# Attention outputs in two passes per block: one head's high and low value parts as weights, its high and low probabilities as the moving side, and the sum of the halves on VectorE

## The chip, the cores and the metric

The kernel runs on one core of a Trainium2 chip. The metric is the device time of one execution in microseconds (us). The three timed runs took 1136.36, 1138.24 and 1138.36 us; their median, 1138.24 us, is the time before.

Engines are named as in the profile: PE is TensorE's matrix multiplication, PEld its loading of weights, DVE is VectorE, ACT is ScalarE, POOL is GpSimd, and SP issues the DMAs.

## What is computed

A windowed attention over 8 batches, 8 heads, 576 positions and 64 features per head, followed by a gated feed-forward layer on the 4608 rows of 512 features:

```python
scores = scale * q @ k.T                   # per batch and head, scale 1/8
mask_plain = (rel >= 0) & (rel < 32)       # heads 0 to 3
mask_dil = (rel >= 0) & (rel < 128) & (rel % 4 == 0)   # heads 4 to 7
attn = softmax(where(mask, scores, -1e9))
out = attn @ v                             # [8, 8, 576, 64]
x = out.transpose(0, 2, 1, 3).reshape(4608, 512)
xn = x / sqrt(mean(x * x) + 1e-6) * rms_g
g = xn @ w_gate;  val = xn @ w_val         # d_ff = 1536
y = (g * sigmoid(g) * val) @ w_out
```

The change concerns the line `out = attn @ v` only.

## The kernel before

The rows are cut into 16 units (u = 0 to 15) of 288 rows, half a batch each. A unit goes through two stages. Its attention comes first: four pairs of heads c, two heads a in each, and per pair three blocks of 96 queries (c = 0, 1, plain window) or four of 72 queries (c = 2, 3, dilated), which are 14 blocks i per unit. Then comes its feed-forward layer: for each of 12 column groups j a gate product (`g`), a value product (`v`) and an output product (into four accumulators `acc`). The attention of a unit is spread over the feed-forward steps of the unit before it, so that TensorE always has large products to run.

**Precision.** Units 0 and 1 multiply in full fp32. From unit 2 on (NNAT = 2) every fp32 number is split in a high and a low part of the type fp32r, and a product is the sum of high by high, high by low and low by high.

**The order of the work** is written out by hand. One step of the loop is one large product (gate, value or output; 12 matmuls of 288 columns for a full one) plus the attention parts that `plan` puts there. `later(dt, rank, fn)` puts a piece of work for the other engines into the step dt ahead, and within a step the pieces are issued by rank. Every engine then runs its own instructions in that order.

**A block's way** (from unit 3 on two steps lie between a block and the next; in unit 2 the blocks come in pairs of neighbouring steps):

1. `scored` (line 499 before): scores into the PSUM bank `s`. 
2. `scores_max` (lines 366 and 371, DVE), `scores_exp` (381, ACT), `scores_norm` (390 and 391, DVE; 397, POOL).
3. `transposed` (469, PE): the probabilities are transposed into the free columns of a bank that also serves gate and value products (`g`, `v`, or a tile `t` of its own in one of these two banks). `untranspose` copies them out in the next step as `pt`, the high part on ACT (452) and the low part on DVE (454). The bank's next product must wait for both.
4. `output` (483, 487, 488, PE): probabilities by values into the bank `o`. Once the opening of the kernel is over there is one such bank.
5. `take` (417, ACT) copies a result from the bank into `xraw`, and `add` (427, DVE, rank 4 of its step) adds another to it. The next block's `output` must wait until the bank has been read.

Before the change the values of both heads are the weights together: `vhi` and `vlo`, [keys, 2 heads x 64]. The moving side holds both heads' probabilities. For a unit of 3 to 15 a block needs two matmuls. Line 487 multiplies `vhi` by high and low probabilities of both heads, 4 x 96 = 384 or 4 x 72 = 288 columns, and line 488 multiplies `vlo` by the high ones of both, 192 or 144 columns, on top of the high half. Of the 128 output rows by all columns only the two blocks in which value head and probability head agree are used. `take` reads the low-probability half of them and `add` the other, two instructions of 64 rows each. In unit 2 a block has three matmuls (line 483) that all add up in the same 192 or 144 columns, `take` alone reads the result, and there is no `add`.

`split_v` makes the value parts, `vhi` on ACT (306) and `vlo` on POOL (310). For unit 2's blocks, DVE also splits the feed-forward weights for the units to come (`split_weight`, lines 247 and 248). Line 349 makes the low part of the queries, 613 that of the layer's input, 676 and 689 are the gate's arithmetic on DVE, 700 and 701 split its result, 723 writes out finished results. The feed-forward products are lines 632, 633 and 634.

## Time and profile before

| What | Value |
|---|---|
| timed runs, median | 1138.24 us |
| profiled execution, first to last instruction | 1137.1 us |
| granted TensorE clock, mean | 0.997 |
| PE busy | 1119.5 us, 98% |
| DVE busy | 795.5 us, 70% |
| ACT busy | 708.7 us, 62% |
| POOL busy | 615.7 us, 54% |
| blocks whose outputs change | 14 in unit 2; 182 in units 3 to 15 (78 of 96 queries, 104 of 72) |

The profile is of a single execution whose span is 1.1 us under the median of the timed runs. A row of a timeline reads: start, duration, engine, line, operation, what is written and read, shape, count, and in brackets how long the engine sat idle before and who ended that. A matmul's duration contains its way through the array, and the next one starts long before it ends. How much of TensorE's time one takes is therefore read from the distance between starts, not from its duration.

### The profile page before, as it was taken

To read this page: it belongs to the slowest core of one execution; us is meant where nothing else is said; L and a number is where in the kernel's file an instruction comes from. 1 tells how busy PE (TensorE), PEld (TensorE's weight loads), DVE (VectorE), ACT (ScalarE), POOL (GpSimd) and SP (SyncE) were. 2 spreads that over 40 slices of the span, in tenths; PEclk is the share of its full clock that TensorE was granted. 3 is DMA by queue.
4 is the path that set the end of the run, shared out by engine and by line. 5 is a ranking of instruction groups with operands and counts; after the bars stand their busy time and mean duration, and the time that the engine had idled before them with its cause. 6 is when DMAs were issued, how large, how long until landed. Compare 5 with 4: busy or idle time off the path is not lost.

```text
span 1137.1 us, 25931 instructions
## 1 busy us (share of the span) xinstructions
PE 1119.5 (98%) x8371; PEld 1088.7 (96%) x8371; DVE 795.5 (70%) x2875; ACT 708.7 (62%) x2608; POOL 615.7 (54%) x1071
## 2 busy tenths in 40 slices
PE   9999889999999999999999999999999999999998
PEld 7787779999999999999999999999999999999998
DVE  6889878858667585876758677675867768586411
ACT  6795665657667566675757666575766757576311
POOL 8223677656556455565646556564655646465311
PEclk9999989999999999999999999999999999999999
DMA  9665221212213031221213122121311212120000
GB/s 246 181 228 198 78 59 40 82 40 71 64 34 98 27 95 42 79 62 31 81 40 103 41 63 74 36 84 39 86 51 54 87 34 79 42 80 15 6 17 22
DMA packets 61545, 82.19 MB, mean 72 GB/s; under 512 B 7298, under 2 KB 41090, under 8 KB 61410
## 3 DMA queue, kind: packets, MB, share of 16 engines
q1 hardware_dynamic: 61410, 80.54, 23.7%
q8 instruction: 67, 1.10, 0.4%
q14 instruction: 68, 0.56, 0.2%
HBM read 71.08 MB, written 9.44 MB: 71 GB/s over the span
## 4 chain that ended last, share of the span: by engine, by line
PE 91%; DVE 5%; ACT 1%; issue 1%; DMA 1%; POOL 1%; POOLq 0%; SPq 0%; ACTq 0%
PE acc L632 9%; PE v L632 8%; PE g L632 8%; PE acc L633 8%; PE acc L634 8%; PE v L633 8%; PE g L633 8%; PE v L634 8%; PE g L634 8%; PE s L499 3%; PE o L487 3%; PE acc L629 2%; PE v L629 1%; PE o L488 1%; PE busy L749 1%; PE g L629 1%
## 5 line engine op out<-in xcount | busy, mean ns | idle before, releaser
L701 POOL TENSOR_TENSOR hlo<-th,hhi 128x288 fp32r<-128x288 f32 x180 | 146.3, 813 | 200.9 <-ACT hhi L700 150.6
L634 PE MATMUL acc<-hhi,lo 128*128 128x288 f32 x720 | 212.6, 295 | 0.0
L397 POOL TENSOR_SCALAR t<-t,sum 72x72 f32<-72x72 f32 (+3 forms) x414 | 153.1, 382 | 69.7 <-DVE sum L391 61.1
L634 PE MATMUL v<-xhi,lo 128*128 128x288 f32 x612 | 180.5, 295 | 0.0
L634 PE MATMUL g<-xhi,lo 128*128 128x288 f32 x612 | 180.3, 295 | 0.0
L700 ACT CAST hhi<-th 128x288 fp32r<-128x288 f32 x180 | 78.1, 434 | 155.7 <-DVE th L689 153.4
L381 ACT ACTIVATE t<-t,sum 96x128 f32<-96x128 f32 (+3 forms) x448 | 166.1, 375 | 11.4 <-DVE sum L371 10.9
L310 POOL TENSOR_TENSOR vlo<-vt,vhi 128x128 fp32r<-128x128 f32 x196 | 94.1, 480 | 107.6 <-ACT vhi L306 92.7
L671 ACT ACTIVATE th<-g 128x288 f32<-128x288 f32 x180 | 73.8, 410 | 106.1 <-PE g L634 86.3
L634 PEld LDWEIGHTS acc<-hhi,lo 128*128 128x128 f32 x720 | 135.9, 189 | 0.0
L427 DVE TENSOR_TENSOR xraw<-o,xraw 64x72 f32<-64x72 f32 (+1 forms) x364 | 99.1, 272 | 50.6 <-ACT xraw L417 44.5
L676 DVE SCALAR_TENSOR_TENSOR th<-th,g 128x288 f32<-128x288 f32 x180 | 80.4, 447 | 68.3 <-ACT th L671 68.3
L634 PEld LDWEIGHTS v<-xhi,lo 128*128 128x128 f32 x612 | 115.4, 189 | 0.0
L634 PEld LDWEIGHTS g<-xhi,lo 128*128 128x128 f32 x612 | 115.2, 188 | 0.0
L632 PE MATMUL g<-xhi,hi_g 128*128 128x288 f32 x357 | 111.0, 311 | 0.1
L632 PE MATMUL acc<-hhi,hi_o 128*128 128x288 f32 x360 | 111.0, 308 | 0.0
L366 DVE TENSOR_TENSOR t<-s,mask 96x256 f32<-96x256 f32 (+3 forms) x196 | 71.5, 365 | 53.5 <-PE s L499 42.6
L689 DVE TENSOR_TENSOR th<-th,v 128x288 f32<-128x288 f32 x180 | 81.4, 452 | 38.0 <-PE v L634 30.1
L633 PE MATMUL acc<-hlo,hi_o 128*128 128x288 f32 x360 | 107.3, 298 | 0.0
L340 POOL TENSOR_TENSOR ks<-qk,ks 128x288 fp32r<-128x288 f32 (+2 forms) x110 | 104.5, 964 | 0.3 <-ACT ks L335 0.3
L417 ACT COPY xraw<-o 64x72 f32<-64x72 f32 (+1 forms) x364 | 94.1, 259 | 11.7 <-PE o L488 9.6
L633 PE MATMUL g<-xlo,hi_g 128*128 128x288 f32 x322 | 94.9, 295 | 0.0
(192 smaller groups left out, 3597.0 us busy)
## 6 DMA issues: line engine op xcount, KB each, us to landing
qk<-in_qk_dram SPq DMA_DIRECT2D x60, 288.0 KB, 2.8
vt<-in_v_dram SPq DMA_DIRECT2D x196, 64.0 KB, 1.9
qk<-in_qk_dram SPq DMA_DIRECT2D x30, 352.0 KB, 3.0
out_dram<-ot SPq DMA_DIRECT2D x64, 144.0 KB, 1.9
qk<-in_qk_dram SPq DMA_DIRECT2D x30, 304.0 KB, 2.8
raw<-in_w_gate_dram SPq DMA_DIRECT2D x12, 512.0 KB, 4.6
raw<-in_w_val_dram SPq DMA_DIRECT2D x12, 512.0 KB, 4.9
raw<-in_w_out_dram SPq DMA_DIRECT2D x12, 512.0 KB, 4.2
```

What stands on the lines that cost most here:

```text
L310: G.tensor_tensor(out=vl, in0=vs.pop(b), in1=vh, op=ALU.subtract)
L340: ek.tensor_tensor(out=ks[:, 1, :nkt], in0=kr, in1=ks[:, 0, :nkt], op=ALU.subtract)
L381: A.activation(out=t[:nq, a, :n], in_=t[:nq, a, :n], func=AF.Exp, scale=-1.0, bias=sm[:nq, a, 0:1], accum_out=sm[:nq, a, 1:2] if u or i % ...
L397: (V if u == 0 and (c, i) > (NC - 1, 0) else G).tensor_scalar(out=t[:nq, a, :n], in0=t[:nq, a, :n], scalar1=sm[:nq, a, 3:4], scalar2=1.0, ...
L417: A.copy(out=to[a * D:(a + 1) * D], in_=o[a * D:(a + 1) * D, (2 + a) * nq:(3 + a) * nq])
L427: V.tensor_tensor(out=to[rows], in0=o[rows, a * nq:(a + 1) * nq], in1=to[rows], op=ALU.add)
L632: PE.matmul(out, wh[:, cc, :], xh, start=start, stop=False)
L633: PE.matmul(out, wh[:, cc, :], xl, start=False, stop=False)
L634: PE.matmul(out, wl[:, cc, :], xh, start=False, stop=stop)
L676: V.scalar_tensor_tensor(out=t, in0=t, scalar=1.0, in1=g, op0=ALU.add, op1=ALU.mult)
L689: V.tensor_tensor(out=t, in0=t, in1=v_ps[:, :U], op=ALU.mult)
L701: G.tensor_tensor(out=lo, in0=t, in1=hi, op=ALU.subtract)
```

## The change

Weights and moving side are paired by head instead of by part. A tile `vhl` holds, for each head, the high and the low values side by side: [keys, 2 heads, 2 parts, 64]. For head a, the weights are its high and low values (128 columns together), and the moving side is its high and its low probabilities, 2 x 96 = 192 or 2 x 72 = 144 columns. The two matmuls of a block, one per head, write disjoint columns of the bank. In the result, rows 0 to 63 belong to the high values and rows 64 to 127 to the low ones. Three of the four quarters are wanted: high by high, high by low and low by high.

`take` copies high values by high probabilities (rows 0 to 63) of each head. `add` adds high values by low probabilities (rows 0 to 63), and then low values by high probabilities (rows 64 to 127 of the bank, added to the same place). It has four DVE instructions per block where there were two, and the second of each head reads what the first has just written. Unit 2 is treated like the later ones: two matmuls in place of three, and four additions in place of none.

```diff
         def hi():
-                vparts[k] = [late[0].tile([P, 2, D], F32R, name=f"v{p}_{k}", bufs=1) for p in ("hi", "lo")]
-            A.copy(out=vparts[k][0], in_=vs[b])
+                vparts[k] = late[0].tile([P, 2, 2, D], F32R, name=f"vhl_{k}", bufs=1)
+            A.copy(out=vparts[k][:, :, 0], in_=vs[b])
...
         def lo():
-            G.tensor_tensor(out=vl, in0=vs.pop(b), in1=vh, op=ALU.subtract)
+            G.tensor_tensor(out=vp[:, :, 1], in0=vs.pop(b), in1=vp[:, :, 0], op=ALU.subtract)
...
     def take(u, c, i, o):
-        if u <= NNAT:
+        if u < NNAT:
...
-                A.copy(out=to[a * D:(a + 1) * D], in_=o[a * D:(a + 1) * D, (2 + a) * nq:(3 + a) * nq])
+                A.copy(out=to[a * D:(a + 1) * D], in_=o[:D, 2 * a * nq:(2 * a + 1) * nq])
...
     def add(u, c, i, o):
-            V.tensor_tensor(out=to[rows], in0=o[rows, a * nq:(a + 1) * nq], in1=to[rows], op=ALU.add)
+            V.tensor_tensor(out=to[rows], in0=o[:D, (2 * a + 1) * nq:(2 * a + 2) * nq], in1=to[rows], op=ALU.add)
+            V.tensor_tensor(out=to[rows], in0=o[D:, 2 * a * nq:(2 * a + 1) * nq], in1=to[rows], op=ALU.add)
...
         def output(a):
-            if o[0] == NNAT:
-                for k, (vp, t) in enumerate(((vh, 0), (vh, 1), (vl, 0))):
-                    PE.matmul(out, vp, pt[:n, t, :, :nq], start=k == 0, stop=k == 2)
-                return
...
-            PE.matmul(both, vh, pt[:n, :, :, :nq], start=True, stop=False)
-            PE.matmul(out, vl, pt[:n, 0, :, :nq], start=False, stop=True)
+            vp = vparts[everything.index(o) % 2]
+            PE.matmul(o_ps[:, 2 * a * nq:2 * (a + 1) * nq].rearrange("d (t q) -> d t q", t=2),
+                      vp[:n, a].rearrange("k t d -> k (t d)"), pt[:n, :, a, :nq], start=True, stop=True)
...
-            if o[0] > NNAT:
+            if o[0] >= NNAT:
                 later(1, 4, lambda: add(*o, o_ps))
```

Lines behind `add` move: 454 becomes 455, 499 becomes 493, and 632 to 634 become 626 to 628. The matmuls of line 481 stand where 487 and 488 did, and the second addition is line 428.

In the rows below, a number that follows a name tells one buffer from another. On PE, in unit 5, the outputs of the second block of its first pair of heads stand between a value product and the scores of a later block. Before:

```order
L634 MATMUL v_0_4816<-xhi_3_4738,lo_708 128x288
L487 MATMUL o_0_1_4830<-pt_0_1_4731,vhi_1320 128x384
L488 MATMUL o_0_1_4830<-pt_0_1_4731,vlo_1321 128x192
L499 MATMUL s_1_2_4829<-ks_2_4527,qs_2_4562 96x256
L499 MATMUL s_1_2_4829<-ks_3_4560,qs_3_4593 96x256
```

And now:

```order
L628 MATMUL v_0_4914<-xhi_3_4834,lo_708 128x288
L481 MATMUL o_0_1_4928<-pt_0_1_4827,vhl_1319 128x192 x2
L493 MATMUL s_1_2_4927<-ks_2_4623,qs_2_4658 96x256
L493 MATMUL s_1_2_4927<-ks_3_4656,qs_3_4689 96x256
L626 MATMUL acc_0_3939<-hhi_11_4830,hi_g_2234 128x288
```

The place is the same; 384 and 192 columns have become twice 192. On DVE, behind that block, the additions stand between the maxima of one later block's scores and the low probabilities (`pt`) of another. Before:

```order
L371 ISA sum_86 96x1
L427 TENSOR_TENSOR xraw_0_4767<-o_0_1_4830,xraw_0_4767 64x96 x2
L390 TENSOR_REDUCE sum_90<-sum_90 96x2
L391 RECIPROCAL sum_90<-sum_90 96x2
L454 TENSOR_TENSOR pt_1_0_4871<-t_0_4864,pt_1_0_4871 128x192
L723 TENSOR_SCALAR ot_1_4877<-acc_1_3869 128x288
```

And now:

```order
L427 TENSOR_TENSOR xraw_0_4863<-o_0_1_4928,xraw_0_4863 64x96
L428 TENSOR_TENSOR xraw_0_4863<-o_0_1_4928,xraw_0_4863 64x96
L427 TENSOR_TENSOR xraw_0_4863<-o_0_1_4928,xraw_0_4863 64x96
L428 TENSOR_TENSOR xraw_0_4863<-o_0_1_4928,xraw_0_4863 64x96
L390 TENSOR_REDUCE sum_90<-sum_90 96x2
L391 RECIPROCAL sum_90<-sum_90 96x2
L455 TENSOR_TENSOR pt_1_0_4971<-t_0_4964,pt_1_0_4971 128x192
```

Everything behind the additions has two more instructions ahead of it. On DVE in unit 2, at its first block, there was no addition between the low probabilities and a weight's low part (`lo`). Before:

```order
L247 CAST hi_v_1543<-f_839 128x512
L454 TENSOR_TENSOR pt_0_2_1568<-t_1_1561,pt_0_2_1568 128x192
L248 TENSOR_TENSOR lo_1506<-f_839,hi_v_1543 128x512
L390 TENSOR_REDUCE sum_88<-sum_88 96x2
L391 RECIPROCAL sum_88<-sum_88 96x2
```

And now:

```order
L455 TENSOR_TENSOR pt_0_2_1565<-t_1_1559,pt_0_2_1565 128x192
L427 TENSOR_TENSOR xraw_0_1568<-o_0_0_1560,xraw_0_1568 64x96
L428 TENSOR_TENSOR xraw_0_1568<-o_0_0_1560,xraw_0_1568 64x96
L427 TENSOR_TENSOR xraw_0_1568<-o_0_0_1560,xraw_0_1568 64x96
L428 TENSOR_TENSOR xraw_0_1568<-o_0_0_1560,xraw_0_1568 64x96
L248 TENSOR_TENSOR lo_1504<-f_839,hi_v_1541 128x512
```

Four additions have moved in ahead of the weight's low part. ACT, POOL and SP have the same instructions in the same order as before, with other shapes on the lines of `split_v` and other places of the bank in `take`.

More of the change, by code (lines that the diff above doesn't have):

```diff
@@ L473, in output @@
             n = blocks[o[2]][3]
[L474 removed]
+            if o[0] < NNAT:
+                if a == 0:
+                    out = o_ps[:, :2 * nq].rearrange("d (a q) -> d a q", a=2)
+                    PE.matmul(out, vs.pop(o)[:n].rearrange("k a d -> k (a d)"), pt[:n, 0, :, :nq], start=True, stop=True)
                 return
[L476 to L488 removed]
+            vp = vparts[everything.index(o) % 2]
+            PE.matmul(o_ps[:, 2 * a * nq:2 * (a + 1) * nq].rearrange("d (t q) -> d t q", t=2),
+                      vp[:n, a].rearrange("k t d -> k (t d)"), pt[:n, :, a, :nq], start=True, stop=True)
         def scored(a):
```

9 lines of the change are left out of this document (1 added, 8 removed).

## The prediction

> **What bounds the kernel now.** I read the page first: the engines' totals, then the chain that ended last.
>
> ```profile
> PE 1119.5 (98%) x8371; PEld 1088.7 (96%) x8371; DVE 795.5 (70%) x2875; ACT 708.7 (62%) x2608; POOL 615.7 (54%) x1071
> PE 91%; DVE 5%; ACT 1%; issue 1%; DMA 1%; POOL 1%; POOLq 0%; SPq 0%; ACTq 0%
> ```
>
> TensorE is the bound, with 91% of the chain, so anything that shortens its work counts at once. But the change pays for this with DVE, which is busy 70% of the span. Whether there is room is decided stage by stage. Next come the busy times by stretches: two early intervals between outputs of unit 5, one of unit 4, and the whole stage of unit 2 (columns: length, then busy time of PE, PEld, DVE, ACT, POOL).
>
> ```profile
> 341.10:345.00 3.90, 3.88 (x30) 3.90 (x31) 3.62 (x16) 1.91 (x8) 1.94 (x4) 1.00 0.72 194
> 345.00:348.90 3.90, 3.90 (x33) 3.90 (x32) 3.37 (x15) 2.79 (x12) 1.90 (x5) 1.00 0.53 175
> 273.90:277.80 3.90, 3.90 (x32) 3.89 (x32) 3.69 (x15) 2.35 (x11) 2.27 (x6) 1.00 0.58 168
> 133.00:182.00 49.00, 43.72 (x314) 41.57 (x313) 39.60 (x115) 33.85 (x126) 38.02 (x57) 0.93 0.19 55
> ```
>
> Where attention is computed DVE is nearly full: 3.62 of 3.90 us, 3.69 of 3.90 us. In unit 2's stage TensorE itself is busy for only 43.72 of 49 us, and the chain there runs over DVE:
>
> ```profile
> by line: DVE lo L248 14.1%; DVE hi_o L247 8.3%; DVE hi_v L247 5.7%; PE acc L632 5.6%; PE acc L633 5.5%; PE acc L634 5.5%; issue 4.7%; DVE t L371 4.3%; DVE pt L454 3.9%; DVE qs L349 3.8%; DVE t L366 3.7%; PE o L483 3.3%; PE v L632 3.2%; PE g
> ```
>
> **What TensorE saves.** The timeline of PE shows a block of 96 queries, one of 72, and one of unit 2. A matmul's share of TensorE is the distance to the next start.
>
> ```profile
> 356.56 0.34 PE L487 MATMUL o<-pt,vhi 128*128 128x384 f32 x1
> 356.73 0.25 PE L488 MATMUL o<-pt,vlo 128*128 128x192 f32 x1
> 356.82 0.35 PE L499 MATMUL s<-ks,qs 128*72 128x208 f32 x2
> ...
> 375.44 0.30 PE L487 MATMUL o<-pt,vhi 104*128 104x288 f32 x1
> 375.58 0.23 PE L488 MATMUL o<-pt,vlo 104*128 104x144 f32 x1
> 375.64 0.35 PE L632 MATMUL acc<-hhi,hi_o 128*128 128x288 f32 x1
> ...
> 181.45 0.34 PE L483 MATMUL o<-pt,vhi 72*128 72x144 f32 x2
> 181.63 0.28 PE L483 MATMUL o<-pt,vlo 72*128 72x144 f32 x1
> 181.74 0.34 PE L632 MATMUL v<-xhi,hi_v 128*128 128x288 f32 x1
> ```
>
> A block of 96 takes 0.17 + 0.09 = 0.26 us now, one of 72 takes 0.14 + 0.06 = 0.20 us. The new matmuls have 192 or 144 columns. By columns alone they would take 0.09 and 0.06 us each. Unit 2's three matmuls of 144 columns show that this isn't so when each has weights of its own to load: 0.18 us for two, 0.11 us for the third, 0.10 us on average. I take 0.11 us for the first of a new pair and the length of line 488's for the second: 0.11 + 0.09 = 0.20 us and 0.11 + 0.06 = 0.17 us. A block of 96 saves 0.06 us, one of 72 saves 0.03 us. Units 3 to 15 have 78 and 104 of them: 4.7 + 3.1 = 7.8 us, or 0.60 us per unit. Unit 2 drops one matmul of 0.10 us in 14 blocks: 1.4 us. The whole saving is 9.2 us.
>
> The Trainium skill, in "TensorE: Matmul & The Clock Gate", section "Back-to-back issue gap", has matmuls follow each other after N columns at 2.4 GHz plus 2.5 ns, with weight loads left aside. By that alone 192 columns would take 82.5 ns and 144 columns 62.5 ns, and an estimate of the saving would be 78 x 0.08 + 104 x 0.06 + 14 x 0.06 = 13.3 us. The trace disagrees for matmuls of unlike weights: 0.10 us at 144 columns.
>
> **What DVE gets.** The existing additions give the price:
>
> ```profile
> L427 DVE TENSOR_TENSOR xraw<-o,xraw 64x72 f32<-64x72 f32 x208 | 59.5, 286 | 46.5 <-ACT xraw L417 43.1
> L427 DVE TENSOR_TENSOR xraw<-o,xraw 64x96 f32<-64x96 f32 x156 | 39.6, 254 | 4.1 <-ACT xraw L417 1.5
> L349 DVE TENSOR_TENSOR qs<-qk,qs 64x288 fp32r<-64x288 f32 x112 | 85.1, 760 | 9.3 <-ACT qs L344 6.3
> ```
>
> Two more per block cost 2 x 0.254 or 2 x 0.286 us. The second of each head reads what the first has just written; such a follower starts some 0.03 us after its forerunner's end (lines 390 and 391 below: 341.01 + 0.15 to 341.20 is 0.04). With 0.07 us for these gaps a block's extra is 0.58 us (96) or 0.64 us (72), 8.6 us per unit and 112 us over 13 units. No addition of before reads rows 64 to 127 for rows 0 to 63. I take line 427's price for it; it can hardly be lower, and the far bound is line 349's 0.76 us, for four times the columns. That bound is too far off to set the range. The copies of `take`, and ACT and POOL making the value parts, keep their number and their size; they are not what DVE waits for at the places below, so I put them at nothing, and at up to 0.1 us per block otherwise.
>
> If TensorE's next reader never came early, all 112 us would lie beside other work. So I look at who reads next. The first place is the bank `o` itself, at unit 5's second block:
>
> ```profile
> 340.45 0.52 DVE L427 TENSOR_TENSOR xraw<-o,xraw 64x96 f32<-64x96 f32 x2
> 341.01 0.15 DVE L390 TENSOR_REDUCE sum<-sum 96x2 f32<-96x4 f32 x1
> 341.20 0.17 DVE L391 RECIPROCAL sum<-sum 96x2 f32<-96x2 f32 x1
> ...
> 340.80 0.29 PE L634 MATMUL v<-xhi,lo 128*128 128x288 f32 x1
> 341.12 0.41 PE L487 MATMUL o<-pt,vhi 128*128 128x384 f32 x1
> ```
>
> The additions end at 340.97 and the matmul starts at 341.12, 0.32 us after its forerunner of 288 columns, which should take 0.14 us (line 487 at 375.44): TensorE waits here already, and the handing over takes 0.15 us. All of 0.58 us counts.
>
> The second kind of place is line 454, queued on DVE right behind the additions. It empties a bank that the next gate or value product needs. Rows of DVE and of the product that waits, in units 5 and 4:
>
> ```profile
> 344.91 0.36 DVE L454 TENSOR_TENSOR pt<-t,pt 128x192 fp32r<-128x192 f32 x1
> 345.51 0.31 PE L632 MATMUL v<-xhi,hi_v 128*128 128x288 f32 x1
> ...
> 348.83 0.36 DVE L454 TENSOR_TENSOR pt<-v,pt 128x192 fp32r<-128x192 f32 x1 [0.39 <-ACT pt L452]
> 349.34 0.36 PE L632 MATMUL g<-xhi,hi_o 128*128 128x288 f32 x1
> ...
> 356.19 0.31 DVE L454 TENSOR_TENSOR pt<-t,pt 104x144 fp32r<-104x144 f32 x1
> 357.01 0.32 PE L632 MATMUL v<-xhi,hi_g 128*128 128x288 f32 x1
> ...
> 367.48 0.31 DVE L454 TENSOR_TENSOR pt<-t,pt 104x144 fp32r<-104x144 f32 x1
> 368.30 0.31 PE L632 MATMUL v<-xhi,hi_v 128*128 128x288 f32 x1
> ...
> 371.51 0.31 DVE L454 TENSOR_TENSOR pt<-v,pt 104x144 fp32r<-104x144 f32 x1 [0.35 <-ACT pt L452]
> 372.07 0.31 PE L632 MATMUL g<-xhi,hi_o 128*128 128x288 f32 x1
> ...
> 277.29 0.35 DVE L454 TENSOR_TENSOR pt<-t,pt 96x192 fp32r<-96x192 f32 x1
> 278.25 0.34 PE L632 MATMUL v<-xhi,hi_v 128*128 128x288 f32 x1
> ...
> 300.17 0.30 DVE L454 TENSOR_TENSOR pt<-t,pt 72x144 fp32r<-72x144 f32 x1
> 300.89 0.34 PE L632 MATMUL v<-xhi,hi_v 128*128 128x288 f32 x1
> ```
>
> The time from line 454's end to the product is spare, less the handing over; between none and 0.15 us I take 0.1 us for that. Unit 5: the spares are 0.24, 0.15, 0.51, 0.51 and 0.25 us. At 348.83 and 371.51 DVE also sat idle for 0.39 and 0.35 us. But it waited for ACT's line 452, and that is itself held up by DVE elsewhere:
>
> ```profile
> ACT pt L452 <- DVE th L689: 92.2, 65, 2.0
> ```
>
> So I count half of that idleness as room. The shortages are 0.58 - 0.14 = 0.44; 0.58 - 0.05 - 0.20 = 0.33; 0.58 - 0.41 = 0.17; 0.64 - 0.41 = 0.23; and 0.64 - 0.15 - 0.18 = 0.31 us. With the first place's 0.58 us unit 5 loses 2.06 us. Unit 4 has no such first place. At 277.29 the spare is 0.61 us, but DVE has been full since the block before (3.69 of 3.90 us), so two blocks' extra arrives: 1.16 - 0.51 = 0.65 us. At 300.17 it is 0.64 - 0.32 = 0.32 us, and two places like 348.83 and 371.51 add 0.64 us: 1.61 us. Odd units (7) and even ones (6) average 1.85 us. Less the saved 0.60 us that is 1.25 us per unit, 16.3 us over 13 units.
>
> In unit 2's stage DVE gets four additions where it had none: 6 x 1.1 us and 8 x 1.23 us with their gaps, 16.4 us. Its room is 49.0 - 39.6 = 9.4 us, so 7.0 us at least don't fit in, and 16.4 us are lost if none of the room lies where it is needed. I take 9 us, near the lower end, since part of the chain there is TensorE's. The saved 1.4 us I count at nothing in a stage where TensorE waits.
>
> **The sum.** The profiled execution's span is 1137.1 us, 1.1 us under the median of 1138.2 us: 1137.1 + 16.3 + 9 + 1.1 = 1163.5, so 1163 us. Differences under 0.2%, about 2.3 us, can't be told from no change in this kernel.
>
> Lower end: the idleness before line 454 is all usable and nothing goes to the handing over. Then unit 5 loses 0.58 + 0.34 + 0.04 + 0.07 + 0.13 + 0.04 = 1.20 us and unit 4 0.55 + 0.04 + 0.22 + 0.04 = 0.85 us, on average 1.04 - 0.60 = 0.44 us per unit, 5.7 us; unit 2 loses 3 us, if DVE makes up some of its 7.0 us behind that stage: 1147 us. Upper end: none of that idleness is usable and the handing over takes 0.15 us everywhere. Unit 5 loses 0.58 + 0.49 + 0.58 + 0.22 + 0.28 + 0.54 = 2.69 us and unit 4 0.70 + 0.58 + 0.37 + 0.54 = 2.19 us, on average 2.46 - 0.60 = 1.86 us per unit, 24.2 us; unit 2 loses 16.4 us: 1179 us. I give 1147 to 1180.
>
> **The rivals.** *DVE's room hides the additions.* DVE is idle for 1137 - 795 = 342 us and gets some 128 us. If its late results still come ahead of TensorE's readers, the saving stands: 1138.2 - 9.2 = 1129 us. For it speaks the average, against it the first place, where TensorE waits already. It decides where a block's extra stays under the spare of 0.15 to 0.5 us, that is at under half of the 0.58 us. Chance 0.04. *The two cancel*, within 2.3 us of before, where the spares just do: 0.03. *DVE becomes the bound of the attention stages*, because each late result also delays ACT, and ACT in turn delays DVE: then a unit loses far more than at the six places, up to all of its 8.6 us. With a third of that beyond the sum above the time is 1163 + 13 x 2.2 = 1192 us, with all of it 1138 + 112 + 16 - 9 = 1257 us. For it speaks the row of ACT waiting for line 689 for 92 us; against it that the later blocks' intervals have room. Chance 0.08.
>
> The forecast, slower with waits at some places of every unit, has the remaining 0.85. Faster by over 0.2%: 0.04. Within 0.2%: 0.03. Slower: 0.85 + 0.08 = 0.93.
>
> **What would show it.** Right: DVE busy at about 795 + 114 = 910 us; the pair of line 481 takes 0.20 us; matmul starts after line 428 and after line 455 come late, by 0.2 to 0.6 us, mostly in the first six blocks of a unit; unit 2's stage is some 9 us longer. Wrong: starts as close together as before at these places, or a gap that lies at other lines.

## The result, and the profile after

The changed kernel takes 1191.17 us (median of 4 runs, 1189.78 to 1192.49), the one before took 1137.82 us in the same comparison. The ratio is 1.0472, with a 95% interval of 1.0457 to 1.0487: slower, by 53 us where 25 were forecast. The profiled executions have spans of 1189.0 and 1137.1 us; the 51.9 us between them are what is explained here. The granted clock is 0.997 in both.

First the page, engines and chain:

```profile
PE 1140.8 (96%) x8357; PEld 1087.0 (91%) x8357; DVE 902.4 (76%) x3295; ACT 703.8 (59%) x2608; POOL 615.6 (52%) x1071
PE 49%; DVE 36%; ACT 8%; issue 5%; POOL 1%; POOLq 0%; DVEq 0%; ACTq 0%
```

DVE has 106.9 us more to do and stands in 36% of the chain instead of 5%. It still is idle for a quarter of the span. So it is not the total that binds, but when its results come.

Where the time lies can be read from the matmuls `rps`, six of which open each unit's feed-forward layer. Here are the first and the last start in the layers of units 2 to 15, the first of which comes right behind the stage with unit 2's attention. Before:

```profile
L539 PE MATMUL rps<-inv,sq x84: 165/224/224, 188.4 to 1062.8; 128*96 128x2 f32 x84
```

and after:

```profile
L533 PE MATMUL rps<-inv,sq x84: 165/224/224, 196.9 to 1114.7; 128*96 128x2 f32 x84
```

The first start is 8.5 us later, which is unit 2's stage, and the last 51.9 us. The 13 stages between, with the attention of units 3 to 15, took 874.4 us and take 917.8 us: 43.4 us more, 3.3 us each. After the last of them nothing is lost. Here is one stage by its busy times (unit 5; length, then PE, PEld, DVE, ACT, POOL), before:

```profile
323.90:391.60 67.70, 67.67 (x531) 67.31 (x529) 48.52 (x184) 43.84 (x165) 39.15 (x69) 1.00 0.21 62
```

After, with an early interval of it and unit 2's stage:

```profile
337.10:408.40 71.30, 69.25 (x531) 67.12 (x529) 56.06 (x212) 43.53 (x165) 39.22 (x69) 1.00 0.20 59
355.20:359.70 4.50, 4.42 (x35) 4.00 (x33) 4.22 (x17) 2.75 (x12) 2.24 (x5) 1.00 0.49 160
133.00:190.40 57.40, 43.64 (x304) 41.27 (x303) 48.83 (x168) 33.87 (x128) 38.58 (x58) 0.94 0.16 47
```

Unit 5's stage is 3.6 us longer for 7.5 us more of DVE. Unit 2's holds nearly the same work of TensorE (43.64 us, 43.72 before) in 57.40 us instead of 49.00.

**What an addition costs.** DVE's groups, by form (busy time and mean ns behind the bar):

```profile
L428 DVE TENSOR_TENSOR xraw<-o,xraw 64x72 f32<-64x72 f32 x224 | 65.1, 290 | 7.7
L427 DVE TENSOR_TENSOR xraw<-o,xraw 64x72 f32<-64x72 f32 x224 | 63.2, 282 | 54.5 <-ACT xraw L417 52.5
L428 DVE TENSOR_TENSOR xraw<-o,xraw 64x96 f32<-64x96 f32 x168 | 43.7, 260 | 5.8
L427 DVE TENSOR_TENSOR xraw<-o,xraw 64x96 f32<-64x96 f32 x168 | 41.9, 249 | 4.3 <-ACT xraw L417 1.4
```

Line 428 costs 8 to 11 ns more than line 427, and 4 to 6 ns more than the forecast took. The price was right. The difference is not that of crossing from one half of the rows to the other, since each line has one head that crosses and one that doesn't. By the mean durations of the trace at 96 columns, line 427 takes 248 ns for the first head (bank rows 0 to 63 into rows 0 to 63) and 251 ns for the second (0 to 63 into 64 to 127), line 428 259 ns (64 to 127 into 0 to 63) and 261 ns (64 to 127 into 64 to 127). Before, the first head (0 to 63 into 0 to 63) took 248 ns and the second (64 to 127 into 64 to 127) 261 ns. So the upper rows cost some 10 ns more than the lower ones, and crossing costs 3 ns at most.

**The first kind of wait: the bank of outputs.** The place of the forecast's 341.12, rows of PE and then of DVE:

```profile
353.96 0.29 PE L628 MATMUL v<-xhi,lo 128*128 128x288 f32 x1
354.92 0.44 PE L481 MATMUL o<-pt,vhl 128*128 128x192 f32 x2 [0.67 <-DVE xraw L428]
355.19 0.40 PE L493 MATMUL s<-ks,qs 128*96 128x256 f32 x2
...
363.19 0.37 PE L481 MATMUL o<-pt,vhl 128*128 128x192 f32 x2
363.39 0.35 PE L493 MATMUL s<-ks,qs 128*72 128x208 f32 x2
364.27 0.37 PE L626 MATMUL g<-xhi,hi_o 128*128 128x288 f32 x1 [0.52 <-DVE pt L455]
```

```profile
353.67 0.25 DVE L427 TENSOR_TENSOR xraw<-o,xraw 64x96 f32<-64x96 f32 x1
...
354.51 0.26 DVE L428 TENSOR_TENSOR xraw<-o,xraw 64x96 f32<-64x96 f32 x1
...
361.41 0.24 DVE L427 TENSOR_TENSOR xraw<-o,xraw 64x96 f32<-64x96 f32 x1
...
362.25 0.26 DVE L428 TENSOR_TENSOR xraw<-o,xraw 64x96 f32<-64x96 f32 x1
...
362.93 0.45 DVE L683 TENSOR_TENSOR th<-th,v 128x288 f32<-128x288 f32 x1
363.76 0.36 DVE L455 TENSOR_TENSOR pt<-v,pt 128x192 fp32r<-128x192 f32 x1 [0.39 <-ACT pt L453]
```

The additions end at 354.77, the matmul starts at 354.92: again 0.15 us for the handing over. It comes 0.96 us behind its forerunner, 0.32 before, so this place costs 0.64 us. A pair of outputs that waits takes 0.27 us (354.92 to 355.19), one that doesn't takes 0.20 us (363.19 to 363.39). The second is what was forecast. The first must be held against the old pair at the same place, which waited too: it took 0.34 us, from 341.12 to the scores at

```profile
341.46 0.40 PE L499 MATMUL s<-ks,qs 128*96 128x256 f32 x2
```

So the new pair is shorter either way, and a pair that has to wait takes some 0.07 us more than one that hasn't, in both kernels. A block that waits now and didn't before saves nothing (0.27 against 0.26 us).

**The second kind: a relay.** The gate product at 364.27 starts 0.88 us after the scores at 363.39. It waited for line 455, that for ACT, and ACT for DVE:

```profile
363.41 0.32 ACT L453 CAST pt<-v 128x192 fp32r<-128x192 f32 x1 [2.36 <-DVE th L683]
```

The same place before, on DVE, ACT and PE (line 454 at 348.83 and the gate product at 349.34 stand in the prediction):

```profile
347.05 0.52 DVE L427 TENSOR_TENSOR xraw<-o,xraw 64x96 f32<-64x96 f32 x2
...
347.98 0.46 DVE L689 TENSOR_TENSOR th<-th,v 128x288 f32<-128x288 f32 x1
```

```profile
348.47 0.32 ACT L452 CAST pt<-v 128x192 fp32r<-128x192 f32 x1 [1.08 <-DVE th L689]
```

```profile
349.15 0.36 PE L499 MATMUL s<-ks,qs 128*72 128x208 f32 x2
```

Set the two against each other. From the first addition to the gate's arithmetic on the value product (line 689, now 683): 0.93 us before, 1.52 after. From there to ACT's copy: 0.49 and 0.48. From there to the low part on DVE: 0.36 and 0.35. From there to TensorE: 0.51 and 0.51. Only the first distance has grown, by 0.59 us, and the others passed it on undiminished. TensorE's own distance has grown by 0.69 us (0.19 to 0.88); 0.06 us of that is the pair of outputs ahead, which has become shorter and so lets TensorE wait longer. The chain is: line 683 reads the value product out of bank `v`; ACT's copy of the probabilities that lie in the same bank follows it; DVE subtracts that copy from the probabilities; only then may TensorE write the next product. The DVE row shows an idle gap of 0.39 us ahead of the low part in both kernels. That gap is the relay's second leg, and no room for work that stands ahead of the first. Over all 65 such places, before:

```profile
L454 DVE TENSOR_TENSOR pt<-v,pt 128x192 fp32r<-128x192 f32 x26 | 9.3, 358 | 10.0 <-ACT pt L452 10.0
L454 DVE TENSOR_TENSOR pt<-v,pt 104x144 fp32r<-104x144 f32 x21 | 6.5, 308 | 7.3 <-ACT pt L452 7.3
L454 DVE TENSOR_TENSOR pt<-v,pt 72x144 fp32r<-72x144 f32 x18 | 5.5, 304 | 6.2 <-ACT pt L452 6.2
```

and after:

```profile
L455 DVE TENSOR_TENSOR pt<-v,pt 128x192 fp32r<-128x192 f32 x26 | 9.3, 358 | 10.0 <-ACT pt L453 10.0
L455 DVE TENSOR_TENSOR pt<-v,pt 104x144 fp32r<-104x144 f32 x21 | 6.5, 308 | 7.3 <-ACT pt L453 7.3
L455 DVE TENSOR_TENSOR pt<-v,pt 72x144 fp32r<-72x144 f32 x18 | 5.5, 303 | 6.2 <-ACT pt L453 6.2
```

The idleness of 10.0, 7.3 and 6.2 us stayed the same. The waits by engine (us in total, times, longest):

```profile
ACT pt L453 <- DVE th L683: 134.0, 65, 3.0
...
PE o L481 <- DVE xraw L428: 16.2, 14, 3.1
...
PE g L626 <- DVE pt L455: 12.6, 26, 0.6
```

Before, the first of these was 92.2 us for the same 65 places, five in each of 13 units. In 52 of them the additions of a block stand ahead of line 683. The Trainium skill, in "PSUM — Partial Sum Buffer", section "PSUM bank collisions raise a hardware error", says that the compiler's scheduler makes any two instructions of different engines depend on each other when they touch the same bank in the same quarter of its partitions, reads among them. The two reads here, line 683 on DVE and line 453 on ACT, stand in that relation, and ACT starts 0.03 us after DVE's end (362.93 + 0.45 = 363.38 to 363.41).

**All places together.** The row of the bank of outputs must not be read as the whole of that wait. Of its 16.2 us, 11.4 us (7 of the 14 times) lie in unit 2's stage, and the view counts only time in which no matmul is under way. The distances between starts show more. From unit 2's layer on, TensorE runs the same groups of matmuls in the same order in both traces; a group is a row of matmuls for one product, for one block's outputs, scores or transposes. So each distance from a group's start to the next can be set against the same one before. For the 13 stages the differences add up as follows, beside what the terms of the forecast's sum had for the same kinds of places (us):

| Kind of place | places, of them over 0.05 us later or longer | forecast | measured |
|---|---|---|---|
| gate product behind scores (the relay) | 65, 36 | 8.3 | 18.3 |
| outputs behind a gate or value product (the bank of outputs) | 117, 57 | 4.1 | 15.5 |
| value product behind scores (line 455 directly behind the additions) | 64, 38 | 11.7 | 8.2 |
| gate and value products that last longer themselves | 117, 47 | 0 | 4.8 |
| outputs that last shorter | 182 | -7.8 | -3.2 |
| everything else | | 0 | -0.1 |
| all (the parts are rounded) | | 16.3 | 43.4 |

The relay takes two places per unit at which 0.50 to 0.72 us are lost, 0.64 us on average, and some of up to 0.21 us. In unit 5 the last late start lies near 372 us of the trace before; what stands behind it, up to the stage's end at 391.60, loses nothing.

### The profile page after: what moved, and what is told of

Read it like the earlier page. It is cut to its first block, busy times and chain, and to the rows that moved or that the text cites. A ratio compares the mean times of both kernels' runs of the same rounds, so it can differ in the third digit from the quotient of the medians.

```text
span 1189.0 us, 26344 instructions
## 1 busy us (share of the span) xinstructions
PE 1140.8 (96%) x8357; PEld 1087.0 (91%) x8357; DVE 902.4 (76%) x3295; ACT 703.8 (59%) x2608; POOL 615.6 (52%) x1071
## 4 chain that ended last, share of the span: by engine, by line
PE 49%; DVE 36%; ACT 8%; issue 5%; POOL 1%; POOLq 0%; DVEq 0%; ACTq 0%
DVE qs L349 6%; PE v L626 5%; PE g L626 5%; PE v L627 4%; PE v L628 4%; PE acc L626 4%; PE g L627 4%; PE g L628 4%; PE acc L627 4%; PE acc L628 4%; DVE th L683 4%; DVE xraw L428 4%; DVE xraw L427 3%; DVE t L371 3%; DVE t L366 3%
## 5 line engine op out<-in xcount | busy, mean ns | idle before, releaser
L427 DVE TENSOR_TENSOR xraw<-o,xraw 64x96 f32<-64x96 f32 (+1 forms) x392 | 105.0, 268 | 58.8 <-ACT xraw L417 53.9
L310 POOL TENSOR_TENSOR vhl<-vt,vhl 128x128 fp32r<-128x128 f32 x196 | 93.3, 476 | 65.5 <-ACT vhl L306 40.6
L428 DVE TENSOR_TENSOR xraw<-o,xraw 64x96 f32<-64x96 f32 (+1 forms) x392 | 108.7, 277 | 13.5
L417 ACT COPY xraw<-o 64x96 f32<-64x96 f32 (+1 forms) x392 | 101.2, 258 | 9.5 <-PE o L481 6.2
L349 DVE TENSOR_TENSOR qs<-qk,qs 64x288 fp32r<-64x288 f32 x112 | 86.2, 770 | 16.5 <-ACT qs L344 13.4
```

The source lines that it names most:

```text
L349: eq.tensor_tensor(out=qs[D:], in0=qr[D:], in1=qs[D:], op=ALU.subtract)
L417: A.copy(out=to[a * D:(a + 1) * D], in_=o[:D, 2 * a * nq:(2 * a + 1) * nq])
L427: V.tensor_tensor(out=to[rows], in0=o[:D, (2 * a + 1) * nq:(2 * a + 2) * nq], in1=to[rows], op=ALU.add)
L428: V.tensor_tensor(out=to[rows], in0=o[D:, 2 * a * nq:(2 * a + 1) * nq], in1=to[rows], op=ALU.add)
```

## Experiments

The theory after the result: DVE's late work reaches TensorE by the relay. The rivals: DVE's load as such, wherever it stands; and the bank of outputs, which is held longer. All differences are medians against the kernel before in the same comparison, in us.

### Which side costs

**e1**: the second addition of each head is left out, and in unit 2 both are. It leaves out low values by high probabilities (in unit 2 also high values by low probabilities), so it is the change on TensorE with DVE's old load.

```diff
-            V.tensor_tensor(out=to[rows], in0=o[D:, 2 * a * nq:(2 * a + 1) * nq], in1=to[rows], op=ALU.add)
...
-            if o[0] >= NNAT:
+            if o[0] > NNAT:
```

> The changed kernel without the second addition of each head (low values by high probabilities is left out of the result), and without any addition in unit 2, so that DVE has the instructions of before and TensorE those of after. If DVE's additions are the whole cost (theory of DVE's lateness), the saving of TensorE is all that is left: 1137.8 - 9.2 = 1129 us, and at most 1132. If the new pairs of matmuls cost TensorE time (theory of the weight loads: two unlike weights for 192 or 144 columns), the time is 1138 us or more, up to half of the loss.

Measured: 1128.51 against 1137.64, ratio 0.9917 (0.9900 to 0.9934), 9.1 us. The forecast's saving of 9.2 us is there when DVE isn't asked for more.

**e2 and e3** are the kernel before with idle additions into a tile that nobody reads, two per block or one, in units 3 to 15.

```diff
+        idle = late[0].tile([P, QB], F32, tag="idle", name=f"idle_{u}_{c}_{i}", bufs=1)
...
             V.tensor_tensor(out=to[rows], in0=o[rows, a * nq:(a + 1) * nq], in1=to[rows], op=ALU.add)
+            V.tensor_tensor(out=idle[rows, :nq], in0=o[rows, a * nq:(a + 1) * nq], in1=to[rows], op=ALU.add)
```

In e3 the idle addition is made for the first head only.

> The kernel before, with two more additions per block in units 3 to 15 that write into a tile nobody reads: DVE has the load of after in these units, TensorE and unit 2 stay as before. Theory of DVE's lateness: units 3 to 15 lose what they lost after, without the saving: 1191.2 - 8.4 (unit 2) + 7.8 = 1190 us. If the pairing by head has a part in the loss (weight loads, reading rows 64 to 127 for rows 0 to 63, a bank written by two matmuls), the time stays clearly under that, 1150 to 1175 us.

Measured: 1183.43, +45.8, ratio 1.0395 (1.0377 to 1.0412). This lies between what the two theories of the expectation had set, some 7 us under the 1190 of DVE's lateness. That figure had added the whole saving of 7.8 us back, of which the changed kernel shows only 3.2.

> The kernel before, with one more addition per block in units 3 to 15 that writes into a tile nobody reads, half the dose. If DVE's room were used up already and each instruction counted (theory of the full engine), half of the loss of units 3 to 15 without the saving, (1190 - 1138) / 2 = 26 us: 1164 us. If spares of 0.15 to 0.5 us at TensorE's readers take the first part of it (the prediction's picture), much less than half: 1145 to 1157 us.

Measured: 1155.19, +17.6, ratio 1.0145 (1.0130 to 1.0161). In units 3 to 15 the loss comes with DVE's additions alone, without the new pairs. The first addition costs 17.6 us and the second 28.2: there is some room, and it is soon used up.

### Moving the work within the order

Three kernels change the order alone. None came down as the theory of the relay asked.

**e4**: the additions of units 3 to 15 a step later.

```diff
-                later(1, 4, lambda: add(*o, o_ps))
+                later(*((2, 0.25) if o[0] > NNAT else (1, 4)), lambda: add(*o, o_ps))
```

> The changed kernel with all four additions of a block (units 3 to 15) put off by one step and queued on DVE behind the next step's product of gate and value and behind the low probabilities. Theory of the place in the queue: TensorE's waits for lines 683 and 455 (0.2 and 0.65 us, some 2.7 us per unit) go, and its waits for the additions stay or grow a little: 1191 - 13 x 2.3 = 1161 us, 1150 to 1170. Theory of the full engine: DVE has as much to do as ever, so 1185 us or more.

Measured: 1266.39, ratio 1.1129 (1.1112 to 1.1145). The waits of TensorE:

```profile
PE o L481 <- DVE xraw L428: 102.9, 162, 3.2
```

TensorE's waits behind the relay are gone, but the bank of outputs now comes free too late in nearly every block (162 times instead of 14).

**e5**: the copies out of the shared bank ahead of the other work of their step, everywhere in units 3 to 15. **e5b**: only where they share the bank with the value product, that is at the 65 places.

```diff
-            later(1, 0.2, lambda: untranspose(t, t_ps))
+            later(1, -0.2 if t[0] > NNAT else 0.2, lambda: untranspose(t, t_ps))
```

```diff
+            later(1, -0.2 if t[0] > NNAT and (now[0] - ends) % 3 == 2 else 0.2, lambda: untranspose(t, t_ps))
```

> The changed kernel, with the transposed probabilities copied out of the bank ahead of the step's product of gate and value, instead of behind it. Theory of the relay: DVE's additions delay the product (line 683), ACT's copy (453) waits for that product since both read one bank, DVE's low part (455) waits for ACT, and TensorE waits for it. Without the first link three waits of 0.65 us per unit shrink by 0.3 to 0.5 us: 13 x 1.2 = 16 us less, 1175 us. Theory of the full engine: the same instructions on DVE, so the same time within 4 us, 1187 to 1195 us.

Measured: 1225.89, ratio 1.0769 (1.0753 to 1.0785), outside both ranges. There is a new wait on ACT:

```profile
ACT th L665 <- DVE pt L455: 46.3, 27, 2.4
```

The gate's tanh reads bank `g`, and now stands behind DVE's low part out of that bank: a relay over the other bank, at 27 places. TensorE loses most elsewhere. By the distances between starts the relay's gate products lose 4.7 us instead of 18.3, but the outputs 45.9 us instead of 15.5.

> The changed kernel, with the transposed probabilities copied out ahead of the product of gate and value only where they share the value product's bank; elsewhere the order is that of the changed kernel. Theory of the relay: the three to four waits of 0.65 us per unit shrink by 0.3 to 0.5 us, and the gate's line 665 gets no new wait: 1175 us, 1168 to 1182. Theory of the full engine: 1187 to 1195 us.

Measured: 1193.27, ratio 1.0495 (1.0470 to 1.0519), no better than the change itself, as the theory of the full engine had it. Its waits:

```profile
ACT pt L453 <- PE v L470: 63.7, 65, 1.4
PE o L481 <- DVE xraw L428: 25.7, 35, 3.2
```

The relay is off the path: ACT's copy now waits for TensorE's transposes instead of line 683. But the additions stand behind what was moved ahead of them, and the waits at the bank of outputs have grown from 16.2 us (14 times) to 25.7 us (35 times). By the distances between starts the relay's gate products lose 4.6 us instead of 18.3, and the outputs 28.3 us instead of 15.5. So the relay isn't the only cause. The theory as first put has failed here: DVE is late in whichever of its results is put last.

### The same load at two places, and the bank

**e10 and e11** are the kernel before with two idle reductions on DVE in each of the 65 steps of the relay. They read no PSUM. In e10 they stand ahead of line 689, in e11 directly behind it. **e12** has them in every block of units 3 to 15, behind the additions, where e2's idle additions held the bank of outputs.

```diff
+    def idle():
+        d = sb.tile([QB, 1], F32, tag="idle", name="idle", bufs=1)
+        for _ in range(2):
+            V.tensor_reduce(out=d, in_=mask, axis=mybir.AxisListType.X, op=ALU.add)
...
+            if t[0] > NNAT and (now[0] - ends) % 3 == 2:
+                later(1, -0.05, idle)
```

In e11 the rank is 0.1 in place of -0.05. In e12 `idle` stands elsewhere:

```diff
                 later(1, 4, lambda: add(*o, o_ps))
+                later(1, 4.01, idle)
```

> The kernel before, with two idle reductions of a constant (0.25 to 0.3 us each) on DVE at 65 places, five per unit from 3 to 15: where a transposed block shares the value product's bank, right ahead of the product of gate and value (line 689). Theory of the relay (product, then ACT's copy 452, then DVE's 454, then TensorE): nearly all of the 0.56 us arrives at TensorE, less the spare of 0.15 to 0.5 us at its end: some 1.3 us per unit, 1138 + 13 to 20 us, 1151 to 1158. If DVE's idle 0.35 us ahead of line 454 is room, about a third of that, 1141 to 1145.

> The same two idle reductions at the same 65 places, one instruction later: behind the product, in the 0.35 us in which DVE waits for ACT's copy. DVE has the same load as in the run before. Theory of the relay: they run beside ACT's copy and cost only what goes beyond 0.35 us and beyond the spare: 1138 to 1142 us. Theory of the full engine: the same as in the run before within 3 us.

Measured: e10 1158.46, +21.1, ratio 1.0180 (1.0167 to 1.0194); e11 1137.12, ratio 1.0000 (0.9991 to 1.0009). The reductions of e10 and ACT's wait for the relay:

```profile
L449 DVE TENSOR_REDUCE idle<-mask 96x1 f32<-96x128 f32 x130 | 35.6, 274 | 2.6
```

```profile
ACT pt L457 <- DVE th L696: 119.1, 65, 2.4
```

Those of e11:

```profile
L449 DVE TENSOR_REDUCE idle<-mask 96x1 f32<-96x128 f32 x130 | 36.2, 279 | 2.2
```

```profile
ACT pt L457 <- DVE th L696: 92.3, 65, 1.9
```

The same 36 us of DVE cost 21.1 us ahead of the relay's first leg and nothing behind it. Ahead of it ACT's wait grows from 92.2 to 119.1 us, behind it stays. Per place that is 0.55 us of work, of which 0.41 us reach ACT and 0.32 us the kernel's time. Of the 20 us in the 13 stages 13.7 us lie at the relay's gate products themselves. This shows the relay, apart from load.

> The kernel before, with two idle reductions of a constant right behind the two additions of each block in units 3 to 15: the same load at the same place as the two idle additions (1183 us), but the bank of the outputs is free before them. If it is lines 454 and 689 behind them that hold TensorE up, 1170 to 1183 us. If holding the bank is the greater part, under 1160 us.

Measured: 1172.95, +35.6, ratio 1.0311 (1.0297 to 1.0326). Against e2's +45.8, with nearly the same time of idle instructions (102.7 us, 96.6 in e2), about 10 us of e2's loss are the holding of the bank itself. That is a balance: the outputs' 16.3 us of e2 have fallen to 0.1, while the value products' 6.2 us have become 13.4.

### Taking load off DVE

**e8**: ACT copies the low values' part out of the bank, and POOL adds it. **e9**: the same with e5b's order.

```diff
+                A.copy(out=low[a * D:(a + 1) * D, :nq], in_=o[D:, 2 * a * nq:(2 * a + 1) * nq])
...
-            V.tensor_tensor(out=to[rows], in0=o[D:, 2 * a * nq:(2 * a + 1) * nq], in1=to[rows], op=ALU.add)
+            G.tensor_tensor(out=to[rows], in0=low[rows, :nq], in1=to[rows], op=ALU.add)
```

> The changed kernel, with the low values' part copied out of the bank by ACT into a tile of its own and added by POOL, so that DVE has two additions per block as before (and two in unit 2). If it is DVE's lateness alone that costs, the saving of TensorE stands but for unit 2: 1128.5 + 4 = 1133 us, 1128 to 1140. If ACT's two copies more (0.5 us per block), in the same relay as DVE's additions, delay the low probabilities as these do, or POOL's slower additions hold up DVE over the shared ports, the time is 1150 to 1180 us.

Measured: 1159.00, ratio 1.0186 (1.0171 to 1.0201). Two of its waits:

```profile
ACT pt L459 <- DVE th L689: 63.2, 65, 1.6
```

```profile
PE t L476 <- POOL t L397: 3.0, 9, 0.5
```

> The last kernel with the order of e5b as well. If the relay over line 683 holds TensorE up there too, up to 5 us less than the last kernel; if there is no wait to take away, the same within 2 us.

Measured: 1168.68, ratio 1.0274 (1.0257 to 1.0291). That is 9.7 us more than e8, where the same or less was expected. Both are better than the change, and neither reaches the kernel before. The relay is not the main reason: ACT's wait for it is shorter than before the change (63.2 us in e8 against 92.2), and the relay's gate products lose 2.8 us of the 14.5 us that the 13 stages lose in e8. TensorE's transposes now wait for POOL's probabilities, which they did not before; POOL is busy for 765.4 us instead of 615.7. That this is what costs was not tried by itself.

**e13**: the low parts of the queries (line 349, 110 instructions, some 77 us of DVE's busy time) are made on POOL. **e17** is the same in the kernel before.

```diff
-                split(*nxt, (1, 2, 2, 3), G, V)
-                split(nxt[0], nxt[1] + 1, (2, 3, 3, 4), G, V)
+                split(*nxt, (1, 2, 2, 3), G, G)
+                split(nxt[0], nxt[1] + 1, (2, 3, 3, 4), G, G)
```

> The changed kernel with the queries' low parts (line 349, 86 us on DVE) made by POOL, so that DVE's total is back to some 816 us, near the 795 us of before. If the total load on DVE decides, most of the loss of units 3 to 15 goes: 1150 to 1160 us. If it is the additions' place ahead of the relay that counts, few of the waits go, since line 349 stands at other places in most steps: 1175 to 1190 us.

Measured: 1150.83, ratio 1.0113 (1.0099 to 1.0127). The page, and ACT's wait for the relay:

```profile
PE 1116.3 (97%) x8357; PEld 1081.3 (94%) x8357; DVE 825.6 (72%) x3185; ACT 705.2 (61%) x2608; POOL 692.4 (60%) x1181
```

```profile
ACT pt L453 <- DVE th L683: 118.8, 65, 2.5
```

With DVE 30 us above the kernel before instead of 107, 40 of the 53 us are gone. This is what the theory of the load asked for, and not that of the relay alone (1175 to 1190). What stays in the later stages is the relay: ACT waits 118.8 us for it, where it was 92.2, and its gate products lose 15.5 us. Outputs and value products start no later than before.

> The kernel before with the queries' low parts on POOL. TensorE hardly waits there in units 3 to 15 (2.2 us for the output's bank), so with either theory 1135 to 1138 us; more than 1140 would mean that POOL, with 89 us more, holds something up.

Measured: 1132.37 against 1137.85, ratio 0.9952 (0.9939 to 0.9964). This is below the 1135 to 1138 expected: room on DVE is worth 5.5 us to the kernel before as well.

**e15** is e13 with e5b's order. **e16** is e13 with unit 2 as before the change (three matmuls by part, no addition). **e14** is both.

```diff
...
+            if o[0] == NNAT:
+                if a == 0:
+                    out = o_ps[:, :2 * nq].rearrange("d (a q) -> d a q", a=2)
+                    for k, (part, t) in enumerate(((0, 0), (0, 1), (1, 0))):
+                        PE.matmul(out, vp[:n, part].rearrange("k a d -> k (a d)"), pt[:n, t, :, :nq], start=k == 0, stop=k == 2)
+                return
...
-            if o[0] >= NNAT:
+            if o[0] > NNAT:
```

> The same without the edit to unit 2. Against 1151 us with the queries' low parts alone moved: if the waits that are left in units 3 to 15 (15.6 us ahead of the gate's products, three per unit) are the relay's, most of them go, 1151 - 13 = 1138 us, 1135 to 1142. If they only move to the output's bank, as they did in the kernel with the low probabilities first and the queries' low parts on DVE, 1148 to 1154.

Measured: 1148.06, ratio 1.0085 (1.0070 to 1.0101).

> The changed kernel with the queries' low parts on POOL and unit 2 as before, without the edit to the low probabilities. Unit 2's stage was 4.8 us longer than before with the former alone; with it taken away 1151 - 4.8 - 1 = 1145 us, 1143 to 1148.

Measured: 1144.30, ratio 1.0058 (1.0045 to 1.0070). Against e13 unit 2 is worth about 7 us.

> The changed kernel with the queries' low parts on POOL, with the low probabilities ahead of the product of gate and value where both share the value product's bank, and with unit 2 as before (three matmuls, no addition). If full stretches of DVE, the relay and unit 2 are the three parts of the loss and nothing else is, each is taken away here and TensorE's saving is left: 1138 - 8 = 1130 us, 1128 to 1135. If a part of the loss comes from elsewhere, the time stays at 1140 us or more.

Measured: 1141.59, ratio 1.0034 (1.0022 to 1.0047). With room, e5b's order helps by 3 us (e13 to e15, e16 to e14), and doesn't remove the rest: e14 missed its 1128 to 1135. The relay's gate products lose 2.0 us there instead of e16's 16.0, but four other kinds of place lose about 2 us each.

### The additions away from the relay

**e18** is e16 with the old pairing by part, and so two additions in place of four, in the blocks 2, 5, 8 and 11 of each unit, whose additions stand ahead of a relay. The other ten blocks (the expectation says eight, which is a slip) keep the pairing per head. **e19** is e18 with the queries' low parts back on DVE.

```diff
+    def by_part(b):
+        return b[0] == NNAT or everything.index(b) % 14 % 3 == 2
...
+            if by_part((u, c, i)):
+                V.tensor_tensor(out=to[rows], in0=o[rows, a * nq:(a + 1) * nq], in1=to[rows], op=ALU.add)
+                continue
...
+            if by_part(o):
+                if a == 0:
+                    vh, vl = (vp[:n, part].rearrange("k a d -> k (a d)") for part in range(2))
+                    both = o_ps[:, :4 * nq].rearrange("d (t a q) -> d t a q", t=2, a=2)
+                    PE.matmul(both, vh, pt[:n, :, :, :nq], start=True, stop=False)
+                    PE.matmul(o_ps[:, :2 * nq].rearrange("d (a q) -> d a q", a=2), vl, pt[:n, 0, :, :nq], start=False, stop=True)
+                return
```

> The kernel after with the queries' low parts on GpSimd, the old products by part in unit 2 and for every third block (those whose additions would stand ahead of a product of the gate that shares its bank with the values' product), and the new pairing per head for the other eight blocks of a unit. Theory of the relay (late product on VectorE, then ScalarE's copy, then VectorE's low part, then TensorE): no addition stands ahead of a relay any more and the full stretches have room, so the saving on TensorE, about 0.4 us in each of 13 units (two thirds of 0.60), comes off the kernel before with the queries' low parts on GpSimd, 1132.4: 1132.4 - 5 = 1127 us, 1125 to 1131. Theory of the load alone (every addition on VectorE costs, wherever it stands): two thirds of the 12 us by which the second addition made the kernel with the old unit 2 longer than the one before it stay, 1132.4 + 8 = 1140 us.

Measured: 1128.52 against 1137.32, ratio 0.9925 (0.9912 to 0.9939). The page, with the chain:

```profile
PE 1108.4 (98%) x8371; PEld 1079.6 (96%) x8371; DVE 789.8 (70%) x3025; ACT 707.1 (63%) x2608; POOL 694.6 (62%) x1181
...
PE 89%; DVE 5%; ACT 2%; DMA 2%; issue 1%; POOL 1%; SPq 0%; POOLq 0%; DVEq 0%; ACTq 0%
```

And ACT's wait for the relay:

```profile
ACT pt L460 <- DVE th L703: 94.1, 65, 2.0
```

> The same mixed pairing, but the queries' low parts stay on VectorE. Theory of the relay with full stretches: the relay has no addition ahead of it, but the stretches in which VectorE is full now still wait at the bank of outputs, so 1140 to 1160 us, with the waits at the first product of the outputs. Theory of the relay alone: 1137.8 - 5 = 1133 us. Theory of the load alone: two thirds of the after kernel's 53 us less unit 2's 8, 1137.8 + 30 = 1168 us.

Measured: 1159.27, ratio 1.0196 (1.0180 to 1.0212). ACT's wait for the relay:

```profile
ACT pt L460 <- DVE th L703: 105.7, 65, 2.3
```

It costs TensorE little there: the relay's gate products lose 1.2 us, the outputs 12.1 and the value products 6.1. This is what the theory of the relay with full stretches had set, 1140 to 1160 us with the waits at the outputs.

The runs with unit 2 as before, or no change at all, as differences from the kernel before:

| Queries' low parts | no block per head | 10 of 14 | all 14 |
|---|---|---|---|
| on DVE | 0 | e19: +22.0 | not run |
| on POOL | e17: -5.5 | e18: -8.8 | e16: +6.5 |

With room on DVE the additions of ten blocks cost little or nothing, and most of TensorE's saving comes out: e18 lies 3.3 us below e17. Counted as in the prediction, ten blocks save 4 x 0.06 + 6 x 0.03 = 0.42 us per unit, 5.5 us. The four blocks ahead of the relay cost 15.3 us more, some 0.3 us at each of 52 places. No run gave the old pairing to four other blocks, but the traces name the place: the relay's gate products lose 16.0 us in e16 and nothing in e18, and no other kind of place loses more than 2 us in either. Without the room the ten blocks alone cost 22 us. e18 is the fastest of all, beside e1, which leaves work out.

## Why the prediction was wrong

The direction was right, and so was the mechanism in the main: TensorE waits for DVE's late results. The size was half of what came, and two terms of the sum were mis-sized for reasons that the runs show.

- **Prices.** TensorE's pairs take 0.20 us and the saving is 9.1 us (e1), against 0.20 and 9.2. An addition costs within 6 ns of the one assumed. DVE is busy for 902 us, against some 910. Right.
- **Unit 2.** 8.5 us against 9. Right.
- **The first place of unit 5.** 0.64 us against 0.58. Right.
- **Half of DVE's idleness ahead of line 454 counted as room.** Wrong, and this is the first step that failed. "So I count half of that idleness as room" gave 0.33 and 0.31 us at the two relay places of unit 5. At the one shown DVE passed on 0.59 us and TensorE lost 0.69; over the 26 such places it lost 0.64 us on average. The number of places was right, their size was half. The 0.39 us stayed in the trace because ACT was late by as much as DVE. With this the relay's term was 8.3 us where 18.3 came. The row of ACT waiting 92 us for line 689 had been read, and its consequence halved. e10 against e11 shows what a delay on this path is worth: 21.1 us against none for the same work.
- **Waits at six places, each with its own block's additions.** Wrong, and the second step, of about the same size. The sum had one place per odd unit at the bank of outputs, 4.1 us; 57 outputs came late, for 15.5 us. Where DVE is full (4.22 of 4.50 us), what is late at one block is still late at the next, and the bank of outputs makes TensorE wait at blocks at which the forecast saw none. e3 and e2 show it: 17.6 us for the first addition, 28.2 for the second. e13 shows it from the other end: 77 us less on DVE give 40 us back. The stages lost 43.4 us, 3.3 us each, where the sum had 1.25. The value products, by contrast, lost less than their term, 8.2 us against 11.7.
- **The saving taken off in full.** The sum had subtracted 0.60 us in every unit, 7.8 us; 3.2 us came out. A pair of 96 queries that doesn't wait is 0.06 us shorter, as forecast, one of 72 queries 0.02 us. But 58 of the 182 pairs wait now, 7 did before, and a wait adds 0.07 us to the pair.
- **Nothing for a product that had to wait.** Gate and value products last up to 0.13 us longer when their start was late, 4.8 us together. The sum had no such term.
- **The rival that was near.** "DVE becomes the bound of the attention stages", with a third of its loss, was put at 1192 us and given 0.08. Its words, that "each late result also delays ACT, and ACT in turn delays DVE", name the relay. That its number fits is luck: the third was assumed, not worked out. What spoke against it was true, since behind 372 us nothing is late in unit 5; but the blocks ahead of that were enough.

The table of places gives 18.3 us to the relay and 15.5 us to the bank of outputs in the changed kernel. These are not what a remedy for one of them would save: each remedy alone moved the wait (e4, e5, e5b), and only with room on DVE do the two come apart. Why the products that waited last longer is open.

## What to carry to other kernels

An idle gap ahead of an instruction is room only if what ended it doesn't itself come from the delayed engine: follow the releaser one step further back before you count it. Price added work by where it stands in the order: ahead of the first leg of a chain over several engines most of it arrives at the end, directly behind that leg none need. When one engine is full in places, first take other work off it; after that a change that failed can pay in the blocks that are off the chain.

## What the runs showed of the hardware

- An addition on DVE that reads one half of a PSUM bank's rows for a result in the other half costs the same within 3 ns as one that stays in its half: 259 against 261 ns from the upper rows, 251 against 248 ns from the lower ones (64x96). Reading the upper rows costs some 10 ns more than reading the lower ones, in both kernels.
- Two matmuls of 192 columns with weights of their own take 0.20 us when they don't wait, and 0.27 to 0.28 us when they had to. Before, the pair of 384 and 192 columns took 0.26 and 0.34 us. That weights aren't loaded ahead in that case would explain it; it was not tried.
